# Attention and expert layer on one core: a plan that models its transfers, loads in halves, and seventy zero products instead of twenty-two

## The chip, the core and the metric

The kernel runs on one core of a Trainium2 chip. A core has five engines that work side by side, each on its own list of instructions in order: TensorE (PE in the profile; PEld is its weight load), VectorE (DVE), ScalarE (ACT), GpSimd (POOL) and SyncE (SP). Here SP issues nearly all transfers. An instruction that waits holds up everything behind it on its engine. The metric is the device time of one execution in microseconds (us), less is better.

## The reference, cut to what matters

```python
# q, k, v: (8 batches, 8 heads, 576 positions, 64); s: (8, 8, 576); all float32
scores = q @ k.T / 8
cum = cumsum(maximum(s, 0))
scores = where(causal, -1e9, scores + minimum(-(cum[i] - cum[j]), 0))
attn = softmax(scores)                      # sum + 1e-9 below
x = (attn @ v) as 4608 tokens x 512
logits = x @ w_gate                         # 8 experts
# each expert takes its 576 best tokens, by one descending order over all logits
out[mask_e] = maximum(x[mask_e] @ w1[e], 0) @ w2[e]
```

## The kernel before, in words

The program has two stages. **Attention** takes the first 345 us or so, then **routing and the eight experts** take the rest. The change touches attention only.

Attention goes over 16 groups (8 batches, two groups of four heads each); a group has two pairs of heads (`pr` 0 and 1). float32 numbers are carried as two float16 parts, so a group needs this preparation:

- `load` (line 343): q and k of the group go from HBM to the float32 tile `raw` (two buffers; L354), 576 KB each. ACT writes the high part into the tile `QK` (four buffers; L379), DVE the low part (L381). Transfers inside SBUF (L386, 72 KB a pair of heads) then move parts to the other half of the partitions. Rows 64 to 66 of `QK` get the running sum of s in three parts (L367): for group 0 straight from the tile `xp`, for the later groups from `auxk` in HBM. For group 0 everything is done pair by pair (`parts`), and ACT writes four more tiles (L388) instead of some moves.
- `vload`: v goes to `rv` (L409, 576 KB), ACT and DVE split it (L412, L414).
- `spass` (line 426): for each pair, nine products of q with k go to PSUM (`pss`, three buffers; L473, L457), and DVE reduces each to row maxima (L442, "reduction" below). ACT and POOL split the maxima (L489, L491, L493), PE transposes them (L495), ACT copies them to `mt` (L497), and a 5 KB transfer puts them into rows 67 and 68 of `QK` (L499, "maxima transfer").
- `sts`: with the maxima in place the score products proper run (`pst`; L514, L515, L517). ACT takes the exponential (L525), POOL its low part (L527). So the first L514 product of a pair cannot begin before its maxima transfer has landed.
- `pv`, `norm`: products with v (L587 to L589), DVE and ACT normalize into `xp` (L602 to L608). `xout` writes a batch's `xp` to HBM (`xs`): one transfer of 1,024 KB and one of 128 KB. `turn` makes the logits.

The first executed work on PE is a chain of products of zeros (L678), with nothing read from them.

The order of all this is not written by hand. `Plan` keeps every step as a `Task` with an engine, a length, its dependencies and a priority. It always starts the task that can begin first by its own clock, and writes the instruction out at that moment. So the numbers of the plan decide only in which order each engine's list stands; on the chip each instruction waits for its real inputs. Before, a transfer's end in the plan was its start, plus `lat` (2.0 in most cases), plus a backlog `self.dma` that each transfer lengthens by its size over 270 KB per us; small ones (`kb=0`) saw no backlog:

```python
self.dma = max(self.dma, t + (1.0 if e == "p" else 0.0)) + x.kb / self.KBUS
x.lat += self.dma - t
```

`consts` prepares tiles. DVE fills the constant rows 64 to 69 of all four `QK` buffers (L270, two instructions a buffer), and a column block is set to zero (L246). `sums` loads s and makes the running sum on DVE (L324 to L333), whose first part is the cast of L327.

## Time and profile before

| what | before |
|---|---|
| time, median of 3 runs | 816.39 us (816.28 to 821.15) |
| the profiled execution | 812.64 us |
| its span in the trace | 810.9 us |
| PE busy / DVE busy / ACT busy / POOL busy | 726.9 / 607.9 / 379.6 / 345.6 us |
| moved by transfers | 119.27 MB, mean 147 GB/s |

The busy times are of the profiled execution. Its own time is 1.74 us above its span and 3.75 us below the median. The shares of a whole span hide that the stages have different limits, so the rows further down are read by stretches.

### The profile page before, as it was taken

How to read it: one execution, taken by the hardware profiler on the slowest of the kernel's cores; microseconds unless marked ns; L12 is line 12 of the kernel's file. 1: busy time of each engine (PE TensorE's matmuls, PEld its weight loads, DVE VectorE, ACT ScalarE, POOL GpSimd, SP SyncE). 2: the span in 40 equal slices, each digit the busy share in tenths (PEclk: the TensorE clock that was granted, in tenths of full speed). 3: DMA queues.
4: the chain of work that ended last, by engine and by line, in shares of the span. 5: the costliest groups of instructions: out<-in, count | busy, mean ns of one | idle time of the engine just before them, and what ended most of it. 6: DMA issues, size and time to landing. Idle time of an engine off the chain costs nothing.

```text
span 810.9 us, 22772 instructions
## 1 busy us (share of the span) xinstructions
PE 726.9 (90%) x8814; PEld 459.3 (57%) x8814; DVE 607.9 (75%) x2070; ACT 379.6 (47%) x724; POOL 345.6 (43%) x425
## 2 busy tenths in 40 slices
PE   4188999999999999824899999999999999999995
PEld 1066788878778888712754545545445454454542
DVE  8768999999999997658888887887878888350110
ACT  3356788878778776602532333432234333341110
POOL 4268788787879887601105031130222114301111
PEclk8578999999999999955999999999999999999998
DMA  4956567686847431013438265393837548931001
GB/s 125 315 163 168 161 196 212 168 238 162 255 135 228 110 102 62 2 59 125 144 118 234 90 162 165 132 232 132 150 124 202 156 143 196 280 117 39 21 21 38
DMA packets 85315, 119.27 MB, mean 147 GB/s; under 512 B 40726, under 2 KB 57238, under 8 KB 85206
## 3 DMA queue, kind: packets, MB, share of 16 engines
q1 hardware_dynamic: 79318, 98.93, 43.3%
q0 software_dynamic: 5888, 18.88, 7.7%
q8 instruction: 69, 1.13, 0.6%
q14 instruction: 40, 0.33, 0.1%
HBM read 71.67 MB, written 19.10 MB: 112 GB/s over the span
## 4 chain that ended last, share of the span: by engine, by line
PE 58%; issue 18%; DVE 12%; DMA 5%; POOL 4%; SPq 1%; ACT 1%; POOLq 0%; another core or an unknown queue 0%; DVEq 0%; ACTq 0%
PE psm L1200 14%; PE psm L1274 13%; DVE scr L442 5%; PE pst L515 4%; PE pst L514 4%; PE pss L473 3%; PE po L587 3%; PE po L589 2%; PE po L588 2%; PE psm L1271 2%; PE psn L1204 2%; POOL out_dram L1254 2%; PE pss L635 1%; PE pss L457 1%; POOL xg L1134 1%
## 5 line engine op out<-in xcount | busy, mean ns | idle before, releaser
L527 POOL TENSOR_TENSOR R<-P 128x512 f16<-128x512 f32 (+1 forms) x224 | 232.8, 1066 | 50.8 <-ACT P L525 49.9
L1200 PE MATMUL psm<-xT,w1p 128*128 128x512 f16 (+1 forms) x876 | 194.1, 353 | 0.0
L1274 PE MATMUL psm<-w2p,hT 128*128 128x512 f16 x768 | 174.7, 379 | 0.0
L525 ACT ACTIVATE P<-pst 128x512 f32<-128x512 f32 (+1 forms) x224 | 119.0, 548 | 50.5 <-PE pst L517 23.2
L1204 PE MATMUL psn<-xT,w1p 128*128 128x64 f16 x768 | 142.2, 193 | 0.0
L442 DVE CUSTOM_DVE_ANT_0 scr<-pss,mS 128x512 bf16<-128x512 f32 (+3 forms) x256 | 124.7, 487 | 16.0 <-PE pss L473 6.4
L1200 PEld LDWEIGHTS <-w1p 128*128 128x128 f16 x876 | 79.7, 98 | 81.6 <-issue 1.4
L1134 POOL DMA_INDIRECT xg<-xs,ids x40 | 42.9, 1072 | 191.7 <-DVE val L824 52.9
L1254 POOL DMA_INDIRECT out_dram<-y,ids x40 | 41.5, 1037 | 183.7 <-ACT y L1285 156.9
L587 PE MATMUL po<-V,P 128*128 128x65 f16 x960 | 113.7, 196 | 2.4 <-DVE xp L608 2.0
L514 PE MATMUL pst<-QK 70*128 70x64 f16 (+4 forms) x512 | 109.0, 252 | 6.8 <-DMA QK<-mt 6.8
L1274 PEld LDWEIGHTS <-hT 128*128 128x128 f16 x768 | 69.0, 98 | 80.4 <-issue 4.0
L589 PE MATMUL po<-V,R 128*128 128x65 f16 x960 | 113.7, 194 | 0.1
L588 PE MATMUL po<-Vl,P 128*128 128x64 f16 x960 | 113.4, 193 | 0.0
L515 PE MATMUL pst<-QK 128*128 128x64 f16 (+4 forms) x512 | 107.6, 251 | 0.0
L1220 ACT ACTIVATE hT<-psm 128x512 f16<-128x512 f32 x64 | 38.2, 597 | 123.5 <-PE psm L1200 103.0
L588 PEld LDWEIGHTS <-P 128*128 128x128 bf16 x960 | 89.9, 99 | 7.8 <-issue 2.8
L587 PEld LDWEIGHTS <-P 128*128 128x128 bf16 x960 | 90.3, 98 | 5.8 <-issue 2.3
L473 PE MATMUL pss<-QK 67*128 67x512 f16 (+3 forms) x256 | 74.1, 311 | 17.6 <-DVE mr L442 10.1
L589 PEld LDWEIGHTS <-R 128*128 128x128 f16 x960 | 89.8, 97 | 0.3 <-POOL R L527 0.3
L1285 ACT ACTIVATE y<-psm 128x512 f32<-128x512 f32 x32 | 19.1, 597 | 122.7 <-PE psm L1274 105.2
L1204 PEld LDWEIGHTS <-w1p 128*128 128x128 f16 x768 | 72.8, 98 | 0.6
(210 smaller groups left out, 1394.1 us busy)
## 6 DMA issues: line engine op xcount, KB each, us to landing
QK<-QK SPq DMA_DIRECT2D x120, 144.0 KB
wst<-in_w_dram SPq DMA_DIRECT2D x32, 512.0 KB
wst<-in_w_dram SPq DMA_DIRECT2D x64, 256.0 KB
rv<-in_v_dram SPq DMA_DIRECT2D x16, 576.0 KB
raw<-in_q_dram SPq DMA_DIRECT2D x15, 576.0 KB
raw<-in_k_dram SPq DMA_DIRECT2D x15, 576.0 KB
xs<-xp SPq DMA_DIRECT2D x8, 1024.0 KB
xs<-xp SPq DMA_DIRECT2D x8, 128.0 KB
```

The costliest lines, as they stand in the source:

```text
L442: return pl.add("v", dur, lambda: nc.vector.tensor_tensor_reduce(scr.t[:, :n], ps(), mask, 1.0, init() if init else -3e38, OP.add, OP.max, ...
L473: nc.tensor.matmul(ps.t[:, :n], F()[:, q0:q0 + 128], F()[:, k0:k0 + n], start=True, stop=True)
L514: nc.tensor.matmul(ps[:, c0:c0 + n], F()[:, ks:ks + 128], F()[:, q:q + n], start=True, stop=False)
L515: nc.tensor.matmul(ps[:, c0:c0 + n], G()[:, ks:ks + 128], G()[:, q:q + n], start=False, stop=not diag)
L525: e = pl.add("a", n / 1200 + 0.171, lambda: nc.scalar.activation(P.t[:, c0:c0 + n], ps.t[:, :n], AF.Exp, scale=1.0 / YS), [x] + fresh, pri ...
L527: sub = lambda eng: eng.tensor_tensor(R.t[:, c0:c0 + n], P.t[:, c0:c0 + n], strided_hi(P.t)[:, c0:c0 + n], op=OP.subtract)
L587: nc.tensor.matmul(o[:, i], H[:, c:c + 128], V.t[:, pr, sl], start=f, stop=False)
L588: nc.tensor.matmul(o[:, i, 0:64], H[:, c:c + 128], Vl.t[:, pr, sl], start=False, stop=False)
L589: nc.tensor.matmul(o[:, i], R.t[:, c:c + 128], V.t[:, pr, sl], start=False, stop=l)
L1200: nc.tensor.matmul(ps[:, tiles[0]:tiles[-1] + 1] if len(tiles) > 1 else ps[:, tiles[0]], lhs(f, c, a), xT.t[:, tiles[0]:tiles[-1] + 1, 4 * ...
L1204: nc.tensor.matmul(pt.t[:, 64 * f:64 * f + 64], lhs(f, c, a), xT.t[:, 4, 4 * b + c, 0:64], start=s, stop=e)
L1274: nc.tensor.matmul(py.t, hT.t[:, f, a, 128 * i:128 * i + 128], w2p.t[:, f, b], start=f == 0 and k == 0, stop=f == 7 and k == 2)
```

## The change

It alters the plan's model and the tasks that it is given:

- **Model of a transfer.** It now begins 0.8 after its issue, takes its size over 270 KB per us behind the backlog, and lands 1.05 later. Small transfers have a size too (2 or 5 KB), so they see the backlog. A task marked `bulk` is not started before the backlog is down to the 0.8 (`DEPTH` is 0). These are numbers of the plan: no wait is added to the program for them.
- **Halves.** q, k and v of a group are loaded by pair of heads: six loads of 288 KB instead of three of 576 KB. The dependency that held group 1's loads (and group 0's v) behind group 0's q moves is gone. `xout` writes five tiles of 256 KB (128 KB the last) instead of two transfers. All these, and the gate weights, are `bulk`.
- **Two engines for issues.** In group 0 the small transfers of L367 and the moves of L386 may be issued by ACT, where the plan has it free earlier; so may the maxima transfers of the first four pairs.
- **Constant rows.** DVE fills them for two `QK` buffers only, the key side first, with the running sum between the two for buffer 0. For the other two buffers POOL copies them by transfer (62 KB in the plan).
- **Zero products.** 70 instead of 22, at priority 50 (last). The plan counts the first 16 at 0.43 and the rest at 0.22.

The core of the diff:

```diff
@@ Plan @@
+    BEGIN, LAND = 0.8, 1.05
+    DEPTH = 0.0
...
+        x.bulk, x.land = bulk, self.LAND if kb and lat is None else None
...
         t = max(x.ready + x.slack, self.free[e])
+        if x.bulk:
+            t = max(t, self.dma - self.BEGIN - self.DEPTH)
...
-            self.dma = max(self.dma, t + (1.0 if e == "p" else 0.0)) + x.kb / self.KBUS
-            x.lat += self.dma - t
+            self.dma = max(self.dma, t + (1.0 if e == "p" else 0.0 if x.land is None else self.BEGIN)) + x.kb / self.KBUS
+            x.lat = self.dma - t + (x.lat if x.land is None else x.land)
@@ consts @@
-            for c in range(2):
-                k["row", i, c] = pl.add("v", 0.85, lambda t=t, c=c: nc.vector.tensor_scalar(
...
+            if i < 2:
+                for c in (1, 0):
+                    made.append(pl.add("v", 0.85, lambda rows=rows, c=c: nc.vector.tensor_scalar(
...
+            else:
...
+                made.append(pl.add("p", 0.9, lambda rows=rows: nc.gpsimd.dma_start(rows, self.r["QK"].slots[1][0][64:70, 0]),
+                                   self.rows1 + [k["QK", 1]], prio=-20, kb=62))
@@ load @@
-        late = self.st[0]["pass"][1][1][:2] if g == 1 else []
-        for a, z in parts:
+        for r in range(2):
             for t in range(2):
-                ld[a, t] = Sy(0.65, lambda a=a, z=z, t=t: d(raw.t[:, t, a:z], srcs[t][b, :, 2 * hf + a:2 * hf + z]), late,
-                              off=(-98 + a if g == 0 else -7) + t / 10, uses=[raw], kb=295 * (z - a))
+                ld[r, t] = Sy(0.5, lambda d, r=r, t=t: d(raw.t[:, t, r], srcs[t][b, :, 2 * hf + r]),
+                              off=(-98 + r if g == 0 else -7) + t / 10 + r / 20, uses=[raw], kb=295, bulk=True)
...
-                aux[p].append(Sy(0.32, lambda p=p, r0=r0, r1=r1, src=src: d(
+                aux[p].append(Sy(0.32 if g else 0.6, lambda d, p=p, r0=r0, r1=r1, src=src: d(
                     QK.t[r0:r1, 0, 1, :, OH * p:OH * p + S], src(p)), [dep] + fresh,
-                    off=-4.5 if g else -90, uses=us))
+                    off=-4.5 if g else -90, uses=us, both=True, kb=2))
@@ spass @@
-        st["max", pr] = pl.add("s", 0.67, lambda: nc.sync.dma_start(
-            QK.t[67:69, 0, 0, pr], mt.t), [x], prio=n0 - 2.9,
-            uses=[mt, QK], lat=2.3)
+        to = QK
+        st["max", pr] = pl.add("s", 0.67, lambda: nc.sync.dma_start(to.t[67:69, 0, 0, pr], mt.t), [x], prio=n0 - 2.9,
+                               uses=[mt, QK], kb=5, alt=("a", 0.62, lambda: nc.scalar.dma_start(
+                                   to.t[67:69, 0, 0, pr], mt.t)) if n0 < 4 else None)
@@ build @@
-        for n in range(22):
-            x = pl.add("t", 0.43, lambda: nc.tensor.matmul(hot.t, zeros[:, 0:128], zeros, start=True, stop=True),
+        for n in range(WARM):
+            x = pl.add("t", 0.43 if n < 16 else 0.22, lambda: nc.tensor.matmul(hot.t, zeros[:, 0:128], zeros, start=True, stop=True),
                        [x, self.k["mZ"]], prio=50, uses=[hot])
```

Every list is newly ordered by this. Three places matter below. The first is the start of ACT's list. Before, it begins with the load of its table and the high parts of q and k of the first pair (`QK_91` and `raw_87` are the buffers of group 0):

```order
L379 ACT_TABLE_LOAD
L379 ACTIVATE QK_91<-raw_87 128x576 [waits DMAHW1_49]
L379 ACTIVATE QK_91<-raw_87 128x576 [waits DMAHW2_49]
L388 ACTIVATE QK_91<-raw_87 64x576 x2
L379 ACTIVATE QK_91<-raw_87 128x576 [waits DMAHW3_49]
```

Now an issue of a running-sum row (`xp_118` holds it), which waits for DVE, stands ahead of the table load:

```order
L393 DMA QK_91<-xp_118 1x2x576 [waits DVE_49]
L405 ACT_TABLE_LOAD
L405 ACTIVATE QK_91<-raw_87 128x576 [waits DMAHW1_49]
L405 ACTIVATE QK_91<-raw_87 128x576 [waits DMAHW2_49]
L393 DMA QK_91<-xp_118 1x2x576 [waits DMAHW4_49,DVE_49]
L415 ACTIVATE QK_91<-raw_87 64x576
L393 DMA QK_91<-xp_118 1x2x576 [waits DMAHW7_49,DVE_49]
L415 ACTIVATE QK_91<-raw_87 64x576
```

So three of the six row issues went from SP to ACT, and the high parts stand behind the first of them. The second place is the first maxima transfer. Before, it stands on SP behind the loads of group 3 (`raw_88`), a load of v and three moves of group 2 (`QK_93`):

```order
L354 DMA raw_88<-in_q_dram 128x1152 [waits DMAHW5_49,DVE_49]
L354 DMA raw_88<-in_k_dram 128x1152 [waits DMAHW6_49,DVE_49]
L367 DMA QK_93<-auxk 3x2x576 [waits DMAHW7_49]
L367 DMA QK_93<-auxk 3x2x576 [waits DMAHW0_49]
L409 DMA rv_89<-in_v_dram 128x1152 [waits DMAHW1_49,DVE_49]
L386 DMA QK_93<-QK_93 64x2x576 [waits DMAHW2_49,Activation_49]
L386 DMA QK_93<-QK_93 64x2x576 [waits DMAHW3_49]
L386 DMA QK_93<-QK_93 64x2x576 [waits DMAHW4_49,Activation_49]
L499 DMA QK_91<-mt_112 2x10x128 [waits DMAHW5_49,Activation_49]
```

Now it stands on ACT, right behind the copy to `mt_112`, and ahead of the first exponential; the high part of group 2's k (`QK_93` from `raw_87`) stands ahead of that copy:

```order
L405 ACTIVATE QK_93<-raw_87 128x2x576 [waits DMAHW7_49,DMAHW3_49]
L515 ACTIVATE mp_110<-mr_105 128x10 [waits DVE_49]
L517 ACTIVATE ms_108<-mr_105 128x10
L405 ACTIVATE QK_93<-raw_87 128x2x576 [waits DMAHW7_49,DMAHW4_49]
L523 ACTIVATE mt_112<-pss_124 20x128 [waits PE_49]
L527 DMA QK_91<-mt_112 2x10x128 [waits Activation_49]
L552 ACTIVATE P_101<-pst_126 128x512 [waits PE_49]
```

The third place is SP's list at the start. Group 1's loads (`raw_88`) now stand among group 0's small transfers, where before group 0's six row issues, six of its moves and the write of `auxk` came ahead of them:

```order
L378 DMA raw_88<-in_q_dram 128x576 x2
L393 DMA QK_91<-xp_118 1x2x576 [waits DMAHW0_49,DVE_49]
L378 DMA raw_88<-in_k_dram 128x576 [waits DMAHW1_49]
L393 DMA QK_91<-xp_118 1x2x576 [waits DMAHW2_49,DVE_49]
L378 DMA raw_88<-in_k_dram 128x576 [waits DMAHW3_49]
L412 DMA QK_91<-QK_91 64x576 [waits DMAHW5_49,Activation_49]
```

On PE the 70 zero products stand as 35 ahead of the first real product, 19 behind the first three, then 1, 2, 9 and 4 among the rest of the first pair's nine products; all 22 stood ahead of the first before.

## Rows read from the trace of the kernel before

**Rows 1.** The page: busy time of the engines over the span, and the granted TensorE clock in 40 slices of 20.3 us, in tenths of full speed.

```profile
PE 726.9 (90%) x8814; PEld 459.3 (57%) x8814; DVE 607.9 (75%) x2070; ACT 379.6 (47%) x724; POOL 345.6 (43%) x425
PEclk8578999999999999955999999999999999999998
```

**Rows 2.** Busy time by stretches of the span. The columns after the stretch and its length are PE, PEld, DVE, ACT and POOL (busy us, and instructions in brackets), the granted clock (1.00 is full speed), the busy share of the DMA engines, and GB/s.

```profile
0.00:17.60 17.60, 8.64 (x30) 3.44 (x31) 14.43 (x38) 6.09 (x9) 8.53 (x26) 0.86 0.38 111
17.60:41.60 24.00, 5.23 (x15) 1.48 (x14) 17.18 (x40) 7.46 (x9) 6.40 (x18) 0.50 1.02 301
41.60:70.00 28.40, 24.84 (x273) 17.20 (x273) 21.39 (x68) 15.99 (x33) 19.45 (x25) 0.74 0.69 186
70.00:100.00 30.00, 29.36 (x548) 23.50 (x546) 27.01 (x101) 22.07 (x48) 24.23 (x27) 0.99 0.49 131
100.00:300.00 200.00, 196.06 (x3827) 161.06 (x3825) 190.88 (x670) 159.17 (x339) 167.92 (x177) 1.00 0.64 186
300.00:345.00 45.00, 40.84 (x885) 34.98 (x883) 30.50 (x104) 28.79 (x65) 31.04 (x36) 1.00 0.09 29
345.00:810.90 465.90, 421.94 (x3247) 217.60 (x3244) 306.46 (x1053) 140.03 (x223) 88.03 (x121) 0.95 0.48 134
```

**Rows 3.** The chain of work that ended last, in its first 80 us: start, length, what was waited for or done.

```profile
21.45 7.45 DMA raw<-in_k_dram
28.92 5.32 DMA QK<-QK
36.36 5.25 DMA QK<-mt
41.65 0.58 PE pst L514
```

**Rows 4.** Instructions in order of time, from 0 to 17.4 us: start, length (of several together where a count above 1 follows), engine (a q marks an issue), line, operation, and in brackets the idle time before it and what ended that.

```profile
0.81 1.28 ACT L379 ACT_TABLE_LOAD   x1 [0.81 <-PEq L1354]
1.49 0.56 SPq L354 DMA_DIRECT2D raw<-in_q_dram  x1
1.60 6.92 PE L678 MATMUL po<-mZ 128*128 128x512 f16 x22 [1.60 <-DVE mZ L246]
3.73 0.70 DVE L324 TENSOR_SCALAR xp<-xp 64x576 f32<-64x576 f32 x1 [1.49 <-DMA xp<-in_s_dram]
4.46 1.67 DVE L270 TENSOR_SCALAR QK<-mZ,vec 6x2560 f16<-6x2560 f16 x2
4.51 0.69 ACT L379 ACTIVATE QK<-raw 128x576 f16<-128x576 f32 x1 [2.42 <-DMA raw<-in_q_dram]
5.52 0.69 ACT L379 ACTIVATE QK<-raw 128x576 f16<-128x576 f32 x1 [0.32 <-DMA raw<-in_k_dram]
5.78 2.26 PEld L678 LDWEIGHTS <-mZ 128*128 128x128 f16 x11 [0.21 <-issue]
6.11 1.24 ACT L388 ACTIVATE QK<-raw 64x576 f16<-64x576 f32 x2
6.16 1.35 DVE L325 TENSOR_TENSOR_SCAN xp<-xp,mZ 64x576 f32<-64x576 f32 x1
7.57 0.48 DVE L246 MEMSET QK<- 128x512 uint32 x1
7.98 0.39 DVE L327 CAST xp<-xp 64x576 f16<-64x576 f32 x1
8.39 1.37 SPq L367 DMA_DIRECT2D QK<-xp  x2
13.18 1.19 SPq L367 DMA_DIRECT2D QK<-xp  x2
14.31 1.67 DVE L270 TENSOR_SCALAR QK<-mZ,vec 6x2560 f16<-6x2560 f16 x2
15.03 0.80 PE L473 MATMUL pss<-QK 67*128 67x256 f16 x3 [6.50 <-DMA QK<-xp]
16.02 0.42 DVE L442 CUSTOM_DVE_ANT_0 scr<-pss,mS 128x256 bf16<-128x256 f32 x1
17.09 0.58 SPq L354 DMA_DIRECT2D raw<-in_q_dram  x1
```

**Rows 5.** The same view, from 17 to 42 us.

```profile
21.46 1.16 ACT L379 ACTIVATE QK<-raw 128x1152 f16<-128x1152 f32 x1 [11.81 <-DMA raw<-in_q_dram]
22.66 1.36 DVE L381 SCALAR_TENSOR_TENSOR QK<-raw,QK 128x1152 f16<-128x1152 f32 x1 [2.89 <-ACT QK L379]
28.03 1.35 DVE L414 SCALAR_TENSOR_TENSOR Vl<-rv,V 128x1152 f16<-128x1152 f32 x1
30.09 0.21 ACT L489 ACTIVATE mp<-mr 128x10 f16<-128x10 f32 x1 [1.74 <-DVE mr L442]
31.64 0.27 ACT L497 ACTIVATE mt<-pss 20x128 f16<-20x128 f16 x1 [0.19 <-PE pss L495]
36.36 0.70 SPq L499 DMA_DIRECT2D QK<-mt  x1
```

**Rows 6.** Busy time by short stretches around the changes of the granted clock, columns as in rows 2.

```profile
12.00:13.00 1.00, 0.00 (x0) 0.00 (x0) 1.00 (x3) 0.00 (x0) 1.00 (x1) 0.76 0.08 20
50.00:51.00 1.00, 0.92 (x23) 0.70 (x20) 0.82 (x5) 0.85 (x3) 1.00 (x2) 0.97 0.00 0
61.00:63.00 2.00, 0.00 (x0) 0.00 (x0) 2.00 (x2) 1.90 (x2) 2.00 (x2) 1.00 0.59 112
64.00:70.00 6.00, 5.97 (x59) 4.28 (x57) 4.89 (x16) 2.32 (x7) 3.91 (x8) 0.50 1.05 261
```

**Rows 7.** Issues of loads, and the use of what they bring, between 120 and 165 us, in order of time as in rows 4.

```profile
126.10 1.70 SPq L354 DMA_DIRECT2D raw<-in_q_dram  x1
139.16 1.15 ACT L379 ACTIVATE QK<-raw 128x1152 f16<-128x1152 f32 x1
...
157.16 1.15 ACT L379 ACTIVATE QK<-raw 128x1152 f16<-128x1152 f32 x1
```

More of the change, by code (lines that the diff above doesn't have):

```diff
@@ L39 @@
 PW = 1536
+WARM = 70
 OH = 704
@@ L85 @@
     __slots__ = ("e", "occ", "lat", "f", "left", "next", "prio", "rank", "uses", "ready", "at", "end", "hold", "kb",
-                 "slack", "lock", "alt")
+                 "slack", "lock", "alt", "bulk", "land")
 class Plan:
@@ L320, in sums @@
         self.auxk = self.dr.tile([3, n, S], F16, name="auxk")
-        ld = pl.add("s", 0.3, lambda: nc.sync.dma_start(s, self.sN), prio=-100, kb=147, lat=1.9,
+        ld = pl.add("s", 0.3, lambda: nc.sync.dma_start(s, self.sN), prio=-100, kb=147,
                     uses=sb)
@@ L342, in load, with Sy @@
         t0, st = 2 * g, self.st[g]
-        d, act, stt = nc.sync.dma_start, nc.scalar.activation, nc.vector.scalar_tensor_tensor
+        act, stt = nc.scalar.activation, nc.vector.scalar_tensor_tensor
         raw, QK = self.buf("raw"), self.buf("QK")
         st["QK"] = QK
-        Sy = lambda dur, f, deps=(), off=0.0, **kw: pl.add("s", dur, f, deps, prio=t0 + off, lat=2.0, **kw)
+        def Sy(dur, f, deps=(), off=0.0, both=False, **kw):
+            return pl.add("s", dur, lambda: f(nc.sync.dma_start), deps, prio=t0 + off,
+                          alt=("a", 0.62, lambda: f(nc.scalar.dma_start)) if both and g == 0 else None, **kw)
         parts = ((0, 1), (1, 2)) if g == 0 else ((0, 2),)
@@ L379, in load @@
             hi = [pl.add("a", dur, lambda t=t, a=a, z=z: act(part(A_, 1, t, t, a, z), raw.t[:, t, a:z], AF.Copy, scale=QS),
-                         [ld[a, t]] + fresh[:1], prio=t0 - 5 + off + t / 10, uses=[raw, QK]) for t in range(2)]
+                         [ld[r, t] for r in range(a, z)] + fresh[:1], prio=t0 - 5 + off + t / 10, uses=[raw, QK]) for t in range(2)]
             lo = [pl.add("v", 0.15 + n * S / 960, lambda t=t, a=a, z=z: stt(
@@ L385, in move @@
             def move(to, fr, deps, o):
-                return Sy(0.58, lambda a=a, z=z: d(part(*to, a, z), part(*fr, a, z)), deps, off=o + off, uses=[QK], kb=72 * n)
+                return Sy(0.6, lambda d, a=a, z=z: d(part(*to, a, z), part(*fr, a, z)), deps, off=o + off, uses=[QK], kb=72 * n,
+                          both=True)
             if g == 0:
                 e1 = [pl.add("a", dur, lambda t=t, a=a, z=z: act(part(E_, 0, t, 0, a, z), raw.t[0:64, t, a:z], AF.Copy,
-                                                                 scale=QS), [ld[a, t]] + fresh[:1],
+                                                                 scale=QS), [ld[r, t] for r in range(a, z)] + fresh[:1],
                              prio=t0 - 4.9 + off + t / 10, uses=[raw, QK]) for t in range(2)]
@@ L614, in xout @@
         r = b * S
-        full = self.xs[r:r + 512].rearrange("(i p) c -> p i c", p=128)
-        pl.add("s", 0.6, lambda: nc.sync.dma_start(full, xp.t[:, 0:4].rearrange("p i a c -> p i (a c)")), deps, prio=prio,
-               uses=[xp], kb=1024, lat=2.0)
-        pl.add("s", 0.5, lambda: nc.sync.dma_start(self.xs[r + 512:r + S], xp.t[0:64, 4].rearrange("p a c -> p (a c)")),
-               deps, prio=prio + 0.1, uses=[xp], kb=128, lat=2.0)
+        for i in range(5):
+            n = 128 if i < 4 else 64
+            pl.add("s", 0.5, lambda i=i, n=n: nc.sync.dma_start(
+                self.xs[r + 128 * i:r + 128 * i + n], xp.t[0:n, i].rearrange("p a c -> p (a c)")), deps, prio=prio + i / 10,
+                uses=[xp], kb=2 * n, bulk=True)
     def turn(self, g, pr):
```

33 lines of the change are left out of this document (22 added, 11 removed).

## The prediction

> **What bounds the kernel now.** The page comes first: PE is busy for 726.9 of 810.9 us, but the row of its clock has 5, 7 and 8 among its first four slices, and a second low stretch where routing begins [rows 1]. So the view by stretches is next [rows 2]. From 100 to 300 us PE is busy for 196.06 of 200 and DVE for 190.88: nothing is to be had there by moving transfers. From 345 us on, the 465.9 us of routing and experts use none of the changed code. What is left is the start. In 17.6 to 41.6 us the DMA engines are busy all the time (share 1.02, 301 GB/s), PE works for 5.23 of 24.0 us, DVE for 17.18, and the clock is at 0.50, the 1.2 GHz level. Over the first 100 us DVE is idle for 100 - (14.43 + 17.18 + 21.39 + 27.01) = 20.0 us.
>
> The chain of waits then says which transfer holds the start up [rows 3]: k of group 1 for 7.45 us, a move for 5.32, and the first maxima transfer for 5.25, whereupon the first score product begins at 41.65. The instructions in order of time add what the chain hides [rows 5]: the maxima were in `mt` at 31.64 + 0.27 = 31.91, but SP issued their transfer at 36.36, 4.45 us later, because it had its list to work off first. And the loads of group 1 were issued only at 17.09, while the bandwidth of the first 17.6 us was mostly unused (share 0.38) [rows 2, 4].
>
> **The change, step by step.** *ACT's start gets slower.* Its list now begins with an issue that waits for the cast. DVE gets there by 3.73 + 0.70 + half of 1.67 + 1.35 + the other half + 0.39 + 0.48 = 8.4 us (the two last are the cast and the zero columns; without these 7.9) [rows 4]. Then come an issue (half of 1.37: 0.69), the table load (1.28), and the first high part begins at 10.3 instead of 4.51. Two high parts at 0.69, an issue, an L388 at 0.62, an issue from 13.0, an L388: done at 14.3. The last row of the running sum was issued from 13.18 before and PE went on at 15.03, 1.85 later; from 13.0 that is 14.9. So the first real product stands where it did, and the 5.8 us lie beside the running sum on DVE. But the high parts of the second pair now end at 15.6 (1.24 for the two), DVE's last low part at 16.4, and behind it stand the two L270 of the second buffer (1.67): the first reduction begins at 18.0 instead of 16.02. Cost 2.0 us.
>
> *The reductions.* Before, they ran from 16.02 to 30.09, where ACT picks up the maxima: 14.07 us [rows 4, 5]. In these lay a wait of 2.89 for group 1's high part, whose loads now land before 17 us, and two L270 of the third buffer (2 x 0.84), which POOL's transfer replaces. 14.07 - 2.89 - 1.68 = 9.5: from 18.0 to 27.5. I take 28.0, for the zero products below.
>
> *The maxima transfer.* ACT's two small steps take 0.4 and the high part of group 2's k that stands ahead of the copy 1.16, the copy 0.27; PE's and POOL's part lies beside this (1.55 us from 30.09 to 31.64). So the issue is at 29.9, right behind the copy: the 4.45 us on SP are gone. The landing is bounded by 1.85 (a row of the running sum) and 5.25 (the same transfer before) [rows 3, 4]. I take 2.3, near the lower, since group 3's loads, 1.15 MB, no longer stand ahead: at 301 GB/s these were 3.8 us. The first score product is at 32.2 (31.7 to 35.2) instead of 41.65: 9.5 us earlier (6.5 to 10).
>
> A rule of the Trainium skill speaks against part of this: "DMA: Bandwidth & Descriptors", section "Issuing engines are not separate DMA queues", says that transfers begun by another engine run on the same 16 DMA engines and save only the sequencer's time. By it the 4.45 us go and the 5.25 may stay: the first score would be at 35.2, which is the upper bound above.
>
> *From there to the steady state.* Not all of the 9.5 need reach the end, and more than 9.5 can, so I count DVE. Up to 100 us it did 80.0 us of work. Four L270 leave it (4 x 0.84 = 3.4): 76.6. By 28.0 it will have been idle for 3.2 (as before to 17.6), 2.0 and 1.0, so 21.8 are done. The other 54.8, at the 190.88 of 200 that it holds later [rows 2], take 57.4. On top come waits like those between 41.6 and 70, where it was idle for 7.0: between nothing and 7.0, and I take 2.6, since the clock will again be low at the first scores but the second stall may go. That ends at 88.0 instead of 100: **12.0 us earlier** (7.6 to 14.6). The count by PE agrees: 9.5 us, and up to 2.0 for the stall at 61 to 63, with half of the 6 to 7 us at 0.50 that follow it [rows 6]: 9.5 to 14.9.
>
> *Zero products.* At full clock one takes 2.26 / 11 = 0.21, at the lower level (6.92 - 2.26) / 11 = 0.42 [rows 4]. The 48 new ones fill time in which PE waits anyway (5.23 of 24.0 busy). 35 ahead of the first product end at 1.6 + 11 x 0.42 + 24 x 0.21 = 11.3. The 19 behind the third take 4.0, to 19.7, just as DVE has finished its three reductions (19.5): nothing lost. The cover is thin, though. Before, the clock fell in the row of 12 to 13, some 4 us after the last zero product at 8.52 [rows 6]; now PE is idle from 11.3 to 14.9. If the clock is down by then, the 19 take 8.0 and DVE waits 4.2.
>
> *Halves, tiles of `xs`.* In the steady state a load is issued 31 us ahead of its use (126.10, for the high part at 157.16; the one at 139.16 reads the other buffer) [rows 7]. Whatever the order or the cutting adds there, some us, is covered. I cost it at nothing; from 31 us on it would show at once, PE having no slack. POOL's two copies of rows lie before its first L527, where it works 6.40 of 24.0 us [rows 2].
>
> Against the halves stands another rule of the Trainium skill, "DMA: Bandwidth & Descriptors", section "Rules for kernel authors": one should coalesce small transfers, with 1 MiB or more per DMA for bandwidth. By it the sum would shrink, as in the rival on halves. The rows of the first two loads, each 288 KB, speak against it: the first was issued at 1.49 and used at 4.51 (3.02), the second released its user at 5.52, 1.01 later, so that in a row they run at some 285 GB/s, near the 301 of the full stretch [rows 2, 4].
>
> **Sum.** ACT's start +2.0, reductions -4.6, POOL's zero products +0.5, maxima transfer -4.5 and -2.9: -9.5 at the first score; -2.5 between there and the steady state; steady state, tail and second stage 0. Altogether -12.0. The profiled execution's 812.64 becomes 800.6 (span 810.9 to 798.9). The median lies 3.75 above that execution, and I put the same on mine: 816.39 - 12.0 = **804.4 us**.
>
> **Rivals.** *Gain partly given back* (0.20): the clock is down at 14.9, so DVE waits 4.2 more, and the maxima transfer lands at its upper bound (2.9 more): 12.0 - 7.1 = 4.9, 811.5 us. For it: the 0.4 us of margin above. Against: PE's first idle gap gets shorter, not longer.
>
> *Halves pay* (0.10): each load bears its 3.02 alone, 2.0 more than in a row. Six more transfers stand ahead of the first maxima: 6 x 2.0 = 12, no change, 816.4 us. Against it the 1.01 above; for it, that nothing shows these loads among small transfers.
>
> *ACT waits for landings* (0.09, the other side): its three move issues of group 0 wait for low parts and for other moves to land, and the split of v, group 1's high parts and the maxima stand behind them. If these landings take 5.32, as in rows 3, instead of 1.85, three of them cost 10.4; with the maxima transfer at 5.25 the first score is at 32.2 + 10.4 + 2.9 = 45.5, 3.9 later than before, and DVE stands with it: 820.3 us. It decides from 9.5 us of such waits on. Against it: fewer bytes are then under way, since group 3's loads come later.
>
> *More* (0.13): the clock stays at 2.4 GHz to the first scores and no stall follows. Then the 2.6 go, and DVE runs at 98% as PE does in rows 2: 76.6 - 21.8 = 54.8 takes 55.9, and the end is at 83.9: 16.1, 800.3 us.
>
> **Chances and range.** The forecast, 9 to 15 us (801.4 to 807.4), has the remaining 0.48. From 798.5 to 813.0 the range holds it, the partly given back case and most of *more*: 0.8. About 1%, 8.2 us, is what a measurement of this kernel can tell from no change. Faster by over 1% (below 808.2): 0.48 + 0.13 and half of the first rival, 0.72. Slower by over 1% (above 824.6) only where ACT's waits come out worse than priced, or something like them lies in the steady state: 0.07. The rest is 0.21.
>
> **What would show it.** In the profile after: ACT's first high part near 10 us; the first reduction near 18, the last near 28; an issue of the maxima transfer on ACT within 0.5 us of the copy, and the first score product at 31.7 to 35.2; DMA share well above 0.38 in the first 17.6 us; DVE idle for some 11 us over its first 88; rows of 100 to 300 and the length of the second stage as before. I am wrong if the first score comes after 36 us, if PE's busy share from 100 us on drops under 0.97, or if the first score is early and the end of attention does not follow.

## The result and the profile after

Foretold were 804.4 us (798.5 to 813.0). The time after is **823.96 us**, median of 8 runs (819.77 to 831.85); the kernel before, run beside it on the same chip, has 816.86 (816.08 to 821.15). The ratio is 1.0074, with an interval from 1.0046 to 1.0101: slower, by about 0.7%. The profiled execution of after is the longest of its eight, 831.85 us (span 830.1), and before's, 812.64, is shorter than all eight of before beside it. So the two profiles stand further apart than the medians, by 19.2 us of span for 7.1 us, and the rows below show after in one of its long executions. A second profile of the same kernel is e10 below.

The page again, PE's busy time and its clock in 40 slices (of 20.75 us), to be held against [rows 1]:

```profile
PE 747.2 (90%) x8862; PEld 470.9 (57%) x8862; DVE 612.8 (74%) x2067; ACT 378.0 (46%) x724; POOL 345.4 (42%) x426
PEclk9699999989999999965599999999999999999998
```

Busy time by the stretches of [rows 2], columns as there (PE, PEld, DVE, ACT, POOL, clock, DMA share, GB/s), and one row for the steady part:

```profile
0.00:17.60 17.60, 14.18 (x57) 5.96 (x58) 14.02 (x36) 5.98 (x9) 5.26 (x23) 1.00 0.67 198
17.60:41.60 24.00, 13.07 (x63) 5.99 (x61) 15.80 (x43) 7.33 (x11) 9.84 (x23) 0.68 0.84 199
41.60:70.00 28.40, 27.52 (x451) 21.10 (x450) 24.80 (x92) 23.55 (x50) 24.31 (x35) 0.97 0.61 180
70.00:100.00 30.00, 26.25 (x486) 21.43 (x484) 25.80 (x84) 18.04 (x40) 22.33 (x23) 0.94 0.58 165
100.00:300.00 200.00, 184.15 (x3391) 147.83 (x3388) 179.71 (x605) 143.07 (x304) 151.72 (x157) 0.97 0.63 180
70.00:300.00 230.00, 210.40 (x3874) 169.26 (x3872) 205.51 (x688) 161.10 (x344) 174.06 (x179) 0.96 0.62 178
```

The first three stretches are better than before: the clock is up (0.68 and 0.97 for 0.50 and 0.74), and without the products of zeros PE has done 57 + 63 + 451 - 70 = 501 products by 70 us, against 30 + 15 + 273 - 22 = 296 [rows 2]. At the 3827 / 200 = 19.1 a us of before's steady part that is 10.7 us ahead. Then it is lost, and more: from 70 to 300 us PE is busy for 210.40 of 230 us, where the kernel before has this row:

```profile
70.00:300.00 230.00, 225.41 (x4373) 184.56 (x4371) 217.89 (x770) 181.25 (x386) 192.15 (x203) 1.00 0.62 178
```

That is 499 products fewer, 26 us at 19.1. So attention ends later although it begins earlier: the last gate products (L645 before, L672 after) run at 346.62 and at 363.37. What follows them takes about as long in both, 463.8 and 466.2 us.

The start in order of time, after, for [rows 4, 5] (L405, L407, L499, L468, L527, L541 are now what L379, L381, L473, L442, L499, L514 were):

```profile
1.61 9.80 PE L705 MATMUL po<-mZ 128*128 128x512 f16 x35 [1.61 <-DVE mZ L255]
10.49 0.68 ACT L405 ACTIVATE QK<-raw 128x576 f16<-128x576 f32 x1
13.55 4.27 PE L705 MATMUL po<-mZ 128*128 128x512 f16 x19
16.66 0.42 DVE L468 CUSTOM_DVE_ANT_0 scr<-pss,mS 128x256 bf16<-128x256 f32 x1
...
29.42 0.20 ACT L515 ACTIVATE mp<-mr 128x10 f16<-128x10 f32 x1
32.02 1.16 ACT L405 ACTIVATE QK<-raw 128x1152 f16<-128x1152 f32 x1 [2.30 <-DMA raw<-in_k_dram]
33.09 0.25 ACT L523 ACTIVATE mt<-pss 20x128 f16<-20x128 f16 x1
33.37 0.70 ACTq L527 DMA_DIRECT2D QK<-mt  x1
36.85 0.59 PE L541 MATMUL pst<-QK 70*128 70x512 f16 x1 [1.26 <-DMA QK<-mt]
```

And the loads in the steady part, after, which answer to [rows 7]: the issue of q, then ACT's first use of it. The bracket is ACT's wait.

```profile
71.71 0.59 SPq L378 DMA_DIRECT2D raw<-in_q_dram  x1
78.16 1.16 ACT L405 ACTIVATE QK<-raw 128x1152 f16<-128x1152 f32 x1 [2.17 <-DMA raw<-in_q_dram]
...
152.23 1.07 SPq L378 DMA_DIRECT2D raw<-in_q_dram  x2
154.91 0.86 SPq L378 DMA_DIRECT2D raw<-in_k_dram  x2
156.64 1.17 ACT L405 ACTIVATE QK<-raw 128x1152 f16<-128x1152 f32 x1 [1.77 <-DMA raw<-in_q_dram]
161.96 1.16 ACT L405 ACTIVATE QK<-raw 128x1152 f16<-128x1152 f32 x1 [2.49 <-DMA raw<-in_k_dram]
163.66 0.41 ACT L633 ACTIVATE xp<-po 128x320 f16<-128x320 f32 x1
164.10 0.49 DVE L635 TENSOR_TENSOR xp<-po,xp 128x320 f16<-128x320 f32 x1 [2.93 <-ACT xp L633]
```

The loads are now issued 6.45 and 4.41 us ahead of their use; of the first, the second half, which the high part needs too, went out only at 73.56. In the second case the chain can be read off: ACT waits 2.49 us for k, `xp` L633 stands behind that on ACT, DVE waits 2.93 us for it. Short stretches show what PE makes of it:

```profile
156.00:160.00 4.00, 4.00 (x98) 3.52 (x95) 3.86 (x17) 2.82 (x6) 2.56 (x5) 1.00 0.89 267
160.00:164.00 4.00, 1.18 (x15) 0.57 (x13) 1.17 (x6) 2.04 (x5) 1.77 (x3) 0.86 0.58 151
164.00:172.00 8.00, 7.91 (x97) 6.11 (x95) 5.52 (x17) 4.82 (x11) 4.62 (x5) 0.50 0.26 58
```

PE has 1.18 us of work in 4.0, and then runs for 8 us at 0.50, the 1.2 GHz level: 97 products, where 98 had just taken 4 us. From 70 to 355 us ACT's waits in this kernel hold these two rows (in total, how often, longest), and before none for a load:

```profile
ACT QK L405 <- DMA raw<-in_q_dram: 6.1, 4, 2.2
ACT QK L405 <- DMA raw<-in_k_dram: 4.9, 4, 2.5
```

All eight of these waits lie between 75 and 183 us. From 200 to 300 us no load is waited for, and still PE is busy for only 93.19 of 100 us, where before has 97.49. So there is a second loss, which these waits are not. Over the same 70 to 355 us one row of PE's own waits has grown, for DVE's reductions; the first line is before's, the second after's:

```profile
PE pss L473 <- DVE mr L442: 1.7, 3, 1.2
PE pss L499 <- DVE mr L468: 7.5, 17, 1.1
```

### The profile page after: what moved, and what is told of

Read it like the earlier page. It is cut to its first block, busy times and chain, and to the rows that moved or that the text cites. A ratio compares the mean times of both kernels' runs of the same rounds, so it can differ in the third digit from the quotient of the medians.

```text
span 830.1 us, 23002 instructions
## 1 busy us (share of the span) xinstructions
PE 747.2 (90%) x8862; PEld 470.9 (57%) x8862; DVE 612.8 (74%) x2067; ACT 378.0 (46%) x724; POOL 345.4 (42%) x426
## 4 chain that ended last, share of the span: by engine, by line
PE 43%; issue 17%; DVE 9%; POOL 3%; DMA 2%; SPq 0%; ACT 0%; POOLq 0%; another core or an unknown queue 0%; DVEq 0%; ACTq 0%
PE psm L1227 14%; PE psm L1301 12%; DVE scr L468 3%; PE psm L1298 2%; PE psn L1231 2%; POOL out_dram L1281 2%; PE pst L542 1%; PE pst L541 1%; POOL xg L1161 1%; PE psa L956 1%; DVE QK L407 1%; PE po L614 1%; PE pss L499 1%; PE po L616 1%; PE po L615 1%
## 5 line engine op out<-in xcount | busy, mean ns | idle before, releaser
L554 POOL TENSOR_TENSOR R<-P 128x512 f16<-128x512 f32 (+1 forms) x224 | 231.0, 1054 | 52.6 <-ACT P L552 50.9
L1227 PE MATMUL psm<-xT,w1p 128*128 128x512 f16 (+1 forms) x876 | 196.3, 358 | 0.0
L552 ACT ACTIVATE P<-pst 128x512 f32<-128x512 f32 (+1 forms) x224 | 117.3, 548 | 46.3 <-PE pst L544 17.1
L468 DVE CUSTOM_DVE_ANT_0 scr<-pss,mS 128x512 bf16<-128x512 f32 (+3 forms) x256 | 124.5, 486 | 16.3 <-PE pss L499 5.7
L1227 PEld LDWEIGHTS <-w1p 128*128 128x128 f16 x876 | 81.7, 100 | 81.5 <-issue 1.2
L541 PE MATMUL pst<-QK 70*128 70x64 f16 (+4 forms) x512 | 108.2, 253 | 1.7 <-DMA QK<-mt 1.3
L615 PEld LDWEIGHTS <-P 128*128 128x128 bf16 x960 | 91.1, 101 | 7.2 <-issue 3.4
L499 PE MATMUL pss<-QK 67*128 67x512 f16 (+3 forms) x256 | 75.0, 310 | 21.7 <-DVE mr L468 11.8
L614 PEld LDWEIGHTS <-P 128*128 128x128 bf16 x960 | 91.4, 99 | 4.8 <-issue 3.0
L1312 ACT ACTIVATE y<-psm 128x512 f32<-128x512 f32 x32 | 19.1, 597 | 125.9 <-PE psm L1301 108.5
L1231 PEld LDWEIGHTS <-w1p 128*128 128x128 f16 x768 | 72.8, 98 | 0.6
```

Source lines behind the costliest of these rows:

```text
L468: return pl.add("v", dur, lambda: nc.vector.tensor_tensor_reduce(scr.t[:, :n], ps(), mask, 1.0, init() if init else -3e38, OP.add, OP.max, ...
L499: nc.tensor.matmul(ps.t[:, :n], F()[:, q0:q0 + 128], F()[:, k0:k0 + n], start=True, stop=True)
L541: nc.tensor.matmul(ps[:, c0:c0 + n], F()[:, ks:ks + 128], F()[:, q:q + n], start=True, stop=False)
L552: e = pl.add("a", n / 1200 + 0.171, lambda: nc.scalar.activation(P.t[:, c0:c0 + n], ps.t[:, :n], AF.Exp, scale=1.0 / YS), [x] + fresh, pri ...
L554: sub = lambda eng: eng.tensor_tensor(R.t[:, c0:c0 + n], P.t[:, c0:c0 + n], strided_hi(P.t)[:, c0:c0 + n], op=OP.subtract)
L614: nc.tensor.matmul(o[:, i], H[:, c:c + 128], V.t[:, pr, sl], start=f, stop=False)
```

## The experiments

Theory A: the plan's hold (`DEPTH`) brings the loads near their use, and their landing holds ACT, through it DVE and PE. Theory B: another part of the change loses the time. Theory C came later: every edit makes the planner find another order, and the order found around late loads is itself worse. Ratios are to the kernel before in the same set; a point is 0.01 of such a ratio. The table comes first; "first score" is the start of the first L541 (L514) product (in e3 and e8 the line numbers are shifted), "PE" its busy time from 70 to 300 us, "wide" the mean in ns of DVE's L407 (L381) from 70 to 340 us, "waits" those of ACT for `raw` from 70 to 355 us.

| kernel | ratio | first score | PE | wide | waits |
|---|---|---|---|---|---|
| before | 1 | 41.65 | 225.41 | 1420 | 0 |
| after | 1.0074 [1.0046, 1.0101] | 36.85 | 210.40 | 1662 | 11.0 |
| e1 DEPTH 4 | 0.9866 [0.9824, 0.9908] | 38.61 | 225.80 | 1476 | 0 |
| e2 no hold | 0.9849 [0.9813, 0.9884] | 42.02 | 225.99 | 1481 | 0 |
| e3 before + hold | 1.0035 [1.0003, 1.0066] | 33.23 | 216.55 | 1570 | 1.3 |
| e4 22 zeros | 1.0017 [0.9981, 1.0054] | 36.25 | 216.02 | 1659 | 6.5 |
| e5 DEPTH 2 | 0.9873 [0.9820, 0.9927] | 37.09 | 225.28 | 1484 | 0 |
| e6 before + zeros | 1.0101 [1.0046, 1.0156] | 43.23 | 219.69 | 1561 | 0 |
| e7 no hold, SP only | 0.9986 [0.9959, 1.0012] | 40.92 | 220.67 | 1632 | 0 |
| e8 whole loads | 1.0027 [1.0000, 1.0055] | 39.29 | 219.40 | 1578 | 1.0 |
| e9 q, k short | 1.0010 [0.9984, 1.0036] | 36.35 | 216.14 | 1649 | 1.0 |
| e10 after again | 1.0094 [1.0056, 1.0132] | 38.06 | 212.41 | 1666 | 7.5 |
| e11 hold at start | 1.0101 [1.0049, 1.0152] | 37.25 | 220.85 | 1671 | 0 |
| e12 zeros short | 1.0159 [1.0120, 1.0198] | 36.35 | 214.12 | 1656 | 5.8 |
| e13 q, k, v short | 0.9999 [0.9969, 1.0030] | 36.44 | 217.53 | 1665 | 0.6 |
| e14 e13 + half R | 0.9864 [0.9818, 0.9911] | 36.96 | 221.80 | 1520 | 1.0 |
| e15 before + half R | 0.9909 [0.9882, 0.9936] | 43.29 | 226.43 | 1504 | 0 |
| e16 DEPTH 1 | 0.9919 [0.9887, 0.9952] | 36.48 | 223.20 | 1480 | 0 |

The runs were made in sets: e1 to e4, e5 to e8, e9 to e12, e13 to e16. Ratios of two sets can be held against each other only roughly: the part behind the last gate products, which no edit touches, took 458.0 to 460.8 us in the last two and 465.1 to 471.3 in the first two. The traces show one and the same order on every engine up to 340 us, the zero products aside, in after, e4, e9, e10, e12, e13 and e14; before and e15 share another.

**The hold taken out or loosened (e1, e2, e5, e16).**

```diff
-    DEPTH = 0.0
+    DEPTH = 4.0      # e1;  1000.0 in e2, 2.0 in e5, 1.0 in e16
```

> DEPTH 4 instead of 0: a bulk load may start while the plan's backlog is up to 4 us longer; all else as in the changed kernel. In its trace from 60 us on, q was issued 4 to 8 us ahead of its first high part up to 200 us (12 or 13 before the change), and ACT waited 11.0 us for q and k from 70 us on (nothing before). Theory A (the hold moved the loads so near to their use that their landing holds ACT, and through it DVE and PE, up): the leads come back to 11 us or more, ACT's waits for q and k from 70 us on go to under 1 us, PE is busy again for over 193 of the 200 us from 100 to 300, and the time is 806 to 814 us, below the kernel before. Theory B (the loss is in the other parts: issues on ACT, more and smaller transfers, a tighter order of all engines): leads may come back, but PE stays under 189 of 200 and the time at 820 us or more.

> DEPTH 1000: no transfer is held back in the plan, the other parts stay. Theory A: ACT does not wait for q and k from 70 us on, and PE is busy for over 193 of the 200 us from 100 to 300; the start is worse than in the changed kernel, since group 2's and 3's loads come ahead of the first maxima transfer again (first score product after 38 us, against 36.85), so 810 to 818 us. Theory B: 820 us or more.

> The changed kernel with DEPTH = 2.0, so that a load may be issued while up to 2 us of transfers still stand in the model's backlog. Theory A (the hold brings the loads near their use, and their landing holds ACT): the leads of the later loads of q are between those of the changed kernel (4 to 12 us) and those at DEPTH 4 (11 to 18 us); ACT's waits for raw from 70 to 355 us fall from 19.4 us to under 4; the time is near that of DEPTH 4, 0.982 to 0.995 of the kernel before. Theory B (another part of the change loses the time): 1.00 to 1.01, as the changed kernel.

> The changed kernel with DEPTH = 1.0. Measured: 1.0074 and 1.0094 at 0, 0.9873 at 2, 0.9866 at 4, 0.9849 without a hold. Theory A: the loss falls with the lead, so ACT's waits for raw from 70 to 355 us are 3 to 10 us and the time 0.992 to 1.004, between 0 and 2. Theory C (each order by itself): no such row need hold; the time may be anywhere from 0.985 to 1.010 with the waits under 3 us.

(The 19.4 us in the third of these, and in e9's below, is a slip, and so are the 15 to 22 us expected for e10: the two rows above sum to 11.0.) One number changed, and the loss turns into a gain of 1.3 to 1.5%, at DEPTH 1 of 0.8%. Without a hold, q is issued and used so:

```profile
133.61 2.18 SPq L378 DMA_DIRECT2D raw<-in_q_dram  x2
147.74 1.15 ACT L405 ACTIVATE QK<-raw 128x1152 f16<-128x1152 f32 x1
```

14.1 us ahead, without a wait, and PE's row from 70 to 300 us is before's:

```profile
70.00:300.00 230.00, 225.99 (x4413) 185.44 (x4411) 218.09 (x761) 183.33 (x389) 192.11 (x204) 1.00 0.60 174
```

So the hold is what loses the time: B as "another part" fell. At DEPTH 1 the ratio lies between those at 0 and at 2, as A has it, but without the waits that A named (0, for 3 to 10); C had left room for both.

**The hold alone, on the kernel before (e3).**

```diff
         t = max(x.ready + x.slack, self.free[e])
+        if e == "s" and x.kb == 590:
+            t = max(t, self.dma - 0.8)
```

> The kernel before with the hold alone: its 576 KB loads of q, k and v of groups 1 to 15 do not start in the plan before its backlog is down to 0.8. Theory A: q's lead falls to about 5 us in many groups, ACT waits for q and k from 70 us on by 5 to 15 us, and the time is 4 to 14 us above the kernel before unless the start gains as much. Theory B: no such waits, and the time within 3 us of the kernel before or below it.

The hold gives 8.4 us at the first score (33.23 for 41.65) and costs PE 8.9 us from 70 to 300 us. So one rule both makes the start and spoils the steady part. But ACT waits for `raw` only 1.3 us here; the loss came another way, in part by this row of PE's waits in the same stretch, which before does not have:

```profile
PE pst L516 <- DMA QK<-mt: 7.1, 4, 2.9
```

Nor does a short lead alone make a wait: from 67 to 135 us q is issued 4.8 to 5.8 us ahead of its use here, four times, and ACT waits for it once, 0.37 us.

**Products of zeros (e4, e6, e12).** e4 sets WARM to 22 in the changed kernel, e6 sets 70 in the kernel before (each 0.43 in its plan, where the change counts 0.22 from the 17th on); e12 cuts the last 48 of the changed kernel from 512 columns to 8, with every order as it is.

> The changed kernel with 22 zero products instead of 70. Theory A: the zero products do not bear on the loss: 821 to 828 us, as the changed kernel (824), and the first score product within 1.5 us of its 36.85. Theory B, in the form that the zero products on PE hold the first reductions up: the first score product over 1.5 us earlier and the time 2 us or more lower.

> The kernel before with 70 in place of 22 products of zeros, and nothing else. If what is left of the gain without a hold (0.985, though its first score, at 42.22 us, is no earlier than before's) comes from the clock at the start: the granted clock of 41.6 to 70 us rises over before's, some 60 to 120 more matmuls of the reference are issued by 70 us (before 296), worth 3 to 6 us at 19.1 a us, and the time is 0.992 to 0.997. If the rest of the change (maxima, transfers by pair, rows) gives it: 0.998 to 1.004, and the count by 70 us stays within 20 of before's.

> The changed kernel, every engine's order as it is, with the last 48 of the 70 products of zeros cut from 512 columns to 8. If the products behind the first reductions cost nothing and hold the clock: the granted clock of 17.6 to 41.6 us falls from 0.68 to 0.50 to 0.60, the first score comes 0 to 1 us later, and the time is 0 to 2 us above that of the changed kernel run beside it. If they stand in the way of the first reductions: the first score comes 1 to 3 us earlier and the time is 1 to 3 us below it.

e4 has the order of the changed kernel and keeps most of the loss (1.0017, against 0.985 without a hold), so the 48 further zeros are not its cause. e6 missed: the clock of 17.6 to 41.6 us rose from 0.50 to 0.86, but the first score came no earlier, and PE lost 5.7 us after 70 us, where not one instruction had been added. What differs there is the order. In e12 the clock of 17.6 to 41.6 us is 0.50 and the first score comes at 36.35, within the 36.35 to 38.06 of the kernels that have this order and all 70 in full: the zeros neither hindered nor helped it. That e12 is 0.65 points above e10, with shorter products in the same order, is not explained; its profiled execution, 812.12 us, is the shortest of its five and cannot show it.

**ACT's issues, and the halves (e7, e8).** e7 is e2 without the second queue; e8 is the changed kernel with q and k in one piece from group 1 on.

```diff
-                          alt=("a", 0.62, lambda: f(nc.scalar.dma_start)) if both and g == 0 else None, **kw)
+                          alt=("a", 0.62, lambda: f(nc.scalar.dma_start)) if False else None, **kw)    # e7; the same at the maxima transfer
...
-        for r in range(2):
+        for r in range(2 if g == 0 else 1):         # e8; r:z instead of r in the transfer
```

> The changed kernel without a hold (DEPTH = 1000.0) and without the second queue: the moves, the rows of group 0 and the transfer of the maxima are all issued on SP. If ACT's queue gains nothing: the same as without a hold, 0.983 to 0.989, and a first score within 1 us of 42.2 us. If it brings what the prediction said of it (transfer of the maxima issued right behind the copy instead of behind SP's loads): the first score comes 3 to 6 us later than 42.2 us and the time is 0.988 to 0.994.

> The changed kernel with the loads of q and k of groups 1 on in one piece each again (590 KB instead of two of 295 KB; v stays split), the hold as in the change. Theory A: the loads are still begun only at an empty backlog, 4 to 10 us ahead of their use, and one piece lands later than two halves would begin to; ACT waits for raw 5 to 20 us from 70 to 355 us, and the time is 1.00 to 1.02. Theory B, the halves themselves (more issues on SP, smaller transfers) lose the time: back to 0.985 to 0.995.

Without the second queue some 1.4 points go (0.9986 for 0.9849, of two sets), yet the first score is earlier (40.92 for 42.02): the prediction's reason for a gain from ACT's issues is not what shows. PE loses 5.3 us after 70 us, where neither kernel has ACT issue a transfer. With whole loads under the hold ACT's waits fall to 1.0 us, against 5 to 20 expected, and still PE reaches only 219.40. Both speak for C beside A.

**Same order, earlier landing (e9, e13, with e10 beside e9).** Here every engine's list stays as it is, and only the bytes shrink (e13 cuts v as well, from 9 columns of 64 to 2).

```diff
-                ld[r, t] = Sy(0.5, lambda d, r=r, t=t: d(raw.t[:, t, r], srcs[t][b, :, 2 * hf + r]),
+                ld[r, t] = Sy(0.5, lambda d, r=r, t=t: d(raw.t[:, t, r, 0:S if g < 5 else S // 4], srcs[t][b, :, 2 * hf + r, 0:S if g < 5 else S // 4]),
```

> The changed kernel, every engine's order as it is, with only a quarter of the columns of q and k loaded from group 5 on (144 of 576; the computation goes on with what stands in the buffer, so the output is not the reference's). The issues stay as late as the hold makes them; only what they bring lands sooner: the four halves are 0.29 MB in place of 1.18 MB, about 3.3 us less at the 270 KB a us at which the 295 KB parts follow one another. Theory A (the landing of the late loads holds ACT, and through it DVE and PE): ACT's waits for raw from 70 to 355 us fall from 19.4 us to under 5, PE is busy at least 189 us of 100 to 300 us (184.15 in the changed kernel), and the time falls to 0.988 to 0.998 of the kernel before. Theory C (the order that the planner finds under the hold is the worse one, whatever lands when): the waits for raw go, others take their place, PE stays under 187 us, and the time is 1.003 to 1.010.

> The changed kernel as it is, on the same chip as the other three of this set. Every theory expects 1.005 to 1.010 of the kernel before, ACT's waits for raw from 70 to 355 us of 15 to 22 us and PE busy 183 to 187 us of 100 to 300 us; it is the base that the two kernels with the same order are read against.

> The changed kernel, every engine's order as it is, with a quarter of the columns of q and k and two ninths of v loaded from group 5 on (the computation goes on with what stands in the buffers, so the output is not the reference's). With q and k short alone, 1.001 of the kernel before was measured (the changed kernel beside it 1.0094), and one wait of 2.1 us for v was left. Landing alone (theory A): with v's landing gone too the time goes on towards that of DEPTH 2, 0.988 to 0.997. The order (theory C): what is left is not in the landings, and the time stays within 0.997 to 1.004; VectorE's 1152 wide instructions of L407 keep a mean over 1.6 us (1.42 us in the kernel before, 1.48 us at DEPTH 2).

With sooner landings ACT's waits for `raw` go from 7.5 to 1.0 us and the ratio from 1.0094 to 1.0010; v adds nothing that shows (0.9999, in another set). So in the set of e9 and e10 landing is worth 0.84 points, near 7 us; the two intervals leave about 0.4 to 1.3. The single executions show how it is paid: the same lists took 811.49 to 822.99 us in e10's ten, and 806.38 to 813.83 in e9's. What is left from e13 to DEPTH 2, 1.3 points across two sets, is not in the landing of q, k or v. PE's waits for DVE's reductions are, with short loads, what they were in after (first line, e13, 70 to 340 us); at DEPTH 2 these are the two lines for it:

```profile
PE pss L499 <- DVE mr L468: 7.5, 18, 1.1
```

```profile
PE pss L483 <- DVE mr L468: 1.9, 3, 1.1
PE pss L499 <- DVE mr L468: 1.0, 4, 0.5
```

With the loads landed early in both, the lists are what is left to differ, so I put this down to the order.

**Hold at the start only (e11).** `bulk` stays for the loads of groups 0 and 1 and for the gate weights.

> The changed kernel with the hold kept for the loads of groups 0 and 1 alone (and not for those of xp), so that the transfer of the maxima still finds short queues, and the later loads go out as their buffers come free. Theory A: the first score stays early (35 to 39 us), ACT's waits for raw after 70 us are under 3 us, PE is busy over 193 us of 100 to 300 us, and the time is the lowest of all, 0.975 to 0.986. If the order found by the planner matters more than what any one part does (theory C): PE is busy 189 to 193 us of 100 to 300 us, as with the products of zeros alone (190.68) and without the second queue (191.31), and the time is 0.987 to 1.002.

Both theories missed the time. From 100 to 300 us PE is busy for 193.35 us, as A has it, but one late landing ahead of that costs what the start had gained:

```profile
65.61 0.60 SPq L436 DMA_DIRECT2D rv<-in_v_dram  x1
67.60 1.77 SPq L323 DMA_DIRECT2D wgf<-in_w_gate_dram  x1
70.73 1.17 ACT L438 ACTIVATE V<-rv 128x1152 f16<-128x1152 f32 x1 [6.01 <-DMA rv<-in_v_dram]
71.64 0.18 DVE L325 TENSOR_SCALAR wgp<-wgf 128x32 f16<-128x32 f32 x1 [5.03 <-DMA wgf<-in_w_gate_dram]
```

ACT waits 6.01 us, DVE 5.03, for loads that are still held (the v is group 1's, by its place in ACT's list), and PE does 87 products from 70 to 80 us at a clock of 0.53, where before does 185 at 0.97. Up to there the mechanism is A's, at another load, and by 100 us PE has done 852 products to before's 844. From 100 to 300 us it does 3709 to before's 3827, with no load waited for: the rest of the loss lies there, and is not A's.

**What the order costs (e14, e15).** In the groups of instructions by line (count, busy us, mean ns), DVE's 1152 wide instruction stands out, here after and e5:

```profile
L407 DVE SCALAR_TENSOR_TENSOR QK<-raw,QK 128x1152 f16<-128x1152 f32 x25 | 41.1, 1662 | 0.0
```

```profile
L407 DVE SCALAR_TENSOR_TENSOR QK<-raw,QK 128x1152 f16<-128x1152 f32 x24 | 35.2, 1484 | 0.0
```

Undisturbed it takes 1.35; in many places of the slower kernels 2.1 to 2.2, beside GpSimd's R<-P (L554; rows in the last section). In after, the 12 that began between 70 and 340 us with no R<-P under way took 1.34 to 1.36 us, and 11 of the 12 that began during one took 1.41 to 2.20. In the 16 rows of the table that keep R<-P whole, those at or under 0.992, and the kernel before, have means up to 1484, the rest 1561 and more; that goes along with the time and does not yet show which makes which. e14 and e15 halve R<-P from group 5 on, in e13's and in before's order:

> As the kernel with all loads short, and GpSimd's subtractions R<-P of L554 cut to half of their columns from group 5 on, every engine's order as it is. If it is GpSimd's work beside VectorE's that stretches the instructions of L407 to 2.1 us (theory C in detail): their mean falls under 1.5 us, PE is busy over 192 us of 100 to 300 us, and the time falls by 0.6 to 1.2 per cent under that of the kernel with short loads alone, while the same cut in the kernel before gains under 0.4 per cent. If GpSimd has nothing to do with it: the mean stays over 1.6 us and both cuts gain the same, under 0.4 per cent.

> The kernel before with GpSimd's subtractions R<-P cut to half of their columns from group 5 on, its order as it is: the control of the cut. Its L381 (the same instruction) has a mean of 1.42 us, near the 1.35 us of an undisturbed one, so there is little to gain: 0.995 to 1.000 if GpSimd's span itself bounds nothing; under 0.993 if the kernel before waits for GpSimd as well.

In e14 the mean falls to 1520, PE's busy time rises by 4.3 us, its wait for the reductions (the L499 row) falls from 7.5 to 4.3 us, and the time falls by 1.35 points to 0.9864. But the control gains 0.9 points as well, with a mean of 1504, where before had 1420. So about 0.45 points are left for the disturbance beside GpSimd that e14 took away, and with these intervals that is not clear of nothing. The rest I read as GpSimd's time itself, which I had taken to bound nothing; no run separates it.

## Why the prediction was wrong

**The step that failed** is "Halves, tiles of `xs`": "In the steady state a load is issued 31 us ahead of its use (126.10, for the high part at 157.16 ...) ... I cost it at nothing". It failed twice. The lead was read wrongly: between the two rows SP issues q once more, and the view holds

```profile
126.10 1.70 SPq L354 DMA_DIRECT2D raw<-in_q_dram  x1
...
144.21 0.59 SPq L354 DMA_DIRECT2D raw<-in_q_dram  x1
```

so the load of 126.10 is that of 139.16, and the lead was 13.06 us, not 31. And the step asked only whether the order or the cutting adds some us to a load; it did not ask what the hold does to the issue. The hold is part of the diff, and it shortened the lead to 6.45 and 4.41 us in the rows above, with 11.0 us of waits on ACT behind it. Where it stayed at 10 us or more from 70 us on (e16, whose shortest is 140.97 to 151.30, and e5, e1, e2) no load was waited for. That "something like them lies in the steady state" stood in the chances, as part of 0.07, without a price. Against e2 the hold, with the order that the planner finds under it, cost 1.0074 - 0.9849 = 0.0225 of the time before, 18 us. The sum's "steady state, tail and second stage 0" failed for the same reason a second time: it put the new order of the steady part at nothing, and from 200 to 300 us, with no load waited for, PE is busy for 93.19 us where before has 97.49.

**The start** was right in kind, too good in size. The first high part at 10.49 (10.3 foretold), 35 zeros to 11.41 (11.3), 19 more for 4.27 (4.0). The first reduction came at 16.66, earlier than 18.0. The last maxima were there at 29.42 instead of some 28. The issue on ACT stands 0.28 us behind the start of the copy, as foretold, but the copy came at 33.09, since the high part of group 2's k ahead of it waited 2.30 us for its load: the step had taken that load for landed. The transfer took 3.48 us from issue to first score, between the bounds of 1.85 and 5.25, where I had taken 2.3. First score 36.85 for 32.2. By the count of products PE was still 10.7 us ahead at 70 us; the sum had 12.0. Two slips in its arithmetic weigh nothing: the way to the cast adds up to 8.3 us, not 8.4, and the chance of "faster by over 1%" to 0.71, not 0.72.

**The rivals.** "ACT waits for landings" had the right mechanism in the wrong place: it priced group 0's moves, and the waits fell on q and k of later groups, eight times between 75 and 183 us. "Halves pay" is not the cause by itself: the halves are in e1, e2 and e5 too. Under the hold they may have a part, since the second half can go out late (73.56 behind 71.71), and e8 with whole loads has 1.0 us of waits for 11.0; its time, 1.0027, is of another order. What the Trainium skill says in "DMA: Bandwidth & Descriptors", section "Rules for kernel authors" (coalesce small transfers, 1 MiB or more per DMA for bandwidth), would have warned of them. Without a hold (e2) the kernel with 288 KB halves runs at 0.9849 of the one with 576 KB loads, so there they cost nothing that shows.

**The tests** that the prediction set itself were the right ones, and all three speak against it. The first score came after 36 us (36.85), PE's busy share from 100 us on fell under 0.97 (184.15 of 200 in the stretch from 100 to 300 us), and the end of attention did not follow the first score.

**What stays open.** Of the 2.0 to 2.2 points between after (or e10) and DEPTH 2, landing explains 0.84 in the one set where it was tested. The rest goes with the order that the planner finds. PE's waits for DVE's reductions show where it is paid; what in the order makes them is open. Part may be DVE's stretched instructions (e14 against e15, some 0.45 points, not clear of nothing). e6 and e7, with no hold at all, lose 5.3 and 5.7 us of PE after 70 us, where only their order differs.

## What to carry to other kernels

Work out the lead of a load (from its issue to its first use, each issue paired with its own use) before and after a change that moves issues; a rule that starts transfers "only when the line is free" helped here where the line was full, at the start (e3: first score 8.4 us earlier), and hurt where the engines were the limit: there an early load cost nothing that shows (e2), and a late one held everything behind it. In a kernel ordered by a planner, an edit of one part reorders all others: a change there is worth what its own part brings only within the spread of orders, here about 1% (an estimate from the 5 to 6 us that PE lost after 70 us in e7 and e6), so test a part with the order held still (same lists, fewer bytes or columns). The best version that these runs point to is the change with DEPTH at 2 or more, or without a hold: 0.985 to 0.987 of the kernel before.
